# Three small moves in a fused recurrent-attention and MLP kernel: reloads behind a store, the order of the first weights, and a step without a filler

## The chip, the cores and the metric

The kernel runs on one core of one Trainium2 chip. The metric is the time of one execution on the device in microseconds (us); the median over runs is compared. Profiles come from one profiled execution, whose own time is given beside its span.

## What is computed

The output mixes two branches of the same input `x` (2048 rows of 512) with a gate per row. Branch A is attention over segments of 32 rows with 8 memory rows that are carried from segment to segment, so its 64 segments must be computed one after the other. Branch B is a two-layer MLP with a layer norm in front.

```python
def _A_ref(x, mem0, Wq, Wk, Wv, Wo, seg_len):   # 32 heads of 128; M = 8, seg_len = 32
    mem = mem0
    for s in range(n_seg):
        h = concatenate([mem, xs], axis=1)      # 40 rows
        q, k, v = h @ Wq, h @ Wk, h @ Wv        # per head
        p = softmax(where(mask, q @ k.T * scale, -1e9))
        o = (p @ v) @ Wo
        mem = o[:, :M, :]
        outs.append(o[:, M:, :])
def _B_ref(x, w1, b1, w2, b2):
    y = _layernorm(x)
    return gelu(y @ w1 + b1) @ w2 + b2          # 512 -> 1376 -> 512
g = sigmoid((x * gate_w).sum(-1))
return g * a + (1 - g) * b
```

## The kernel before

Everything runs under a manual schedule: the order in which the program calls the instructions is the order on each engine, and the only freedom left is how long each engine waits for the others. Loads that SyncE issues stand in its queue in program order; a wait in front of one holds up all behind it.

**First stage, the MLP (0 to about 86 us).** x is cut into 16 tiles of 128 rows, taken in 8 blocks of two. A block has 11 units `fc`, one for each 128 of the 1376 hidden columns. `a_mm(blk, fc)` does the first layer of a unit: four matmuls into one of two PSUM banks in turn (`SbF` for even units, `W` for odd ones), and a gelu on ScalarE, with the bias column of `b1_sb`, into `hTm`. `b_mm(blk, fc)`, issued two units later (`LAG = 2`), multiplies that with the unit's slice of w2. `prep(blk)` computes the layer norm on VectorE, and `prep_tr` transposes the result `y` on PE; for block 1 this needs the loads of x2 and x3, and its transposes stand behind units 8 and 9 of block 0. The first block also needs w1 in three pieces (units 0 to 2, 3 to 6, 7 to 10: the loads of lines 328, 336 and 337) and w2 (units 0 to 2 and 3 to 5 on ScalarE's queue, line 333; units 6 to 9 by line 339 on SyncE's). Before the first unit PE runs warm-up matmuls on the identity matrix (`warm`, line 521): 13 before the transposes of y, 2 behind them. Then comes the transpose of the bias `b1r` into bank `W` (line 529) and VectorE's copy into `b1_sb` (line 530).

For six of the 16 tiles (`DEF`) the second layer is put off: `spill` stores their gelu results to DRAM (`h_dr`), in 11 pieces of 128 x 128 for each tile.

**The loop (about 86 to 760 us): 64 steps, one for each segment.** A step projects q, k and v (lines 127, 146), computes scores (265, 269) and exponentials (773, 784), sums them over a head's rows with a matrix of ones (`msum`: lines 276, 279), normalises (`mnorm`), multiplies with v (`av`: lines 289, 294), projects with Wo (`wo_pass`: line 158) and takes the new memory rows out of it (`new_mem`: line 728 on PE, 730 on VectorE). Four steps `si` = 0 to 3 make a tile `T`.

Work that doesn't depend on the recurrence fills PE between these parts. Fillers are generators: `run(n)` takes n pieces of the step's own filler (`side`), and `next(mlp)` takes half a unit of the second layer that was put off. `mlp_halves` (line 659 of the profile) multiplies one 128 x 128 piece `hm` of `h_dr` with w2 in two halves of four matmuls into bank `W`; every step takes two halves, one between the matmuls of v and `msum(1)`, one behind `run(W1)`. In step 2, which has no other filler, `mlp_units(7)` takes seven whole units besides, at the places of `run`.

The pieces are loaded by `hm_load` (line 638, SyncE) into five buffers: four ahead of the loop, and one more each time a unit is done, from inside `mlp_halves`. In step 2 four more come with one load into a buffer of another kind (`hm_load4`), which isn't replaced. The two loads of each step that the normalisation of the other rows needs are issued in `recip_x`: the reciprocals `R` are stored to DRAM (`r_dr`, line 699), and read back, spread over all partitions, into `Rb` (line 700); the second waits for the first. One step later POOL multiplies with `Rb` (`x_norm`, line 712) into `UT`, which that step's `wo_pass` reads.

Of the kernel before, what the change touches and what calls it, by code (L numbers as in the profile page):

```python
# [10 lines left out]
BF16 = mybir.dt.bfloat16  # L11
# [16 lines left out]
def kernel(ctx, tc, A_x, A_mem0, A_Wq, A_Wk, A_Wv, A_Wo, A_seg_len, B_x, B_w1, B_b1, B_w2, B_b2, gate_w, out):  # L28
    nc = tc.nc
    P = 128  # L30
# [10 lines left out]
    FC = (F + P - 1) // P  # L41
# [20 lines left out]
    ident = pers.tile([P, P], BF16)  # L62
    g_all = pers.tile([P, NT], FP32)
    omg = pers.tile([P, NT], FP32)
    w2_sb = pers.tile([P, FC, Dm], BF16)
# [147 lines left out]
    def wo_left(T, bk):  # L213
        for n in range(NW):
            wo_group(bk, UL[T % 2], n)
            if n < NW - 1:
                yield

        def ca():
            wl = cw.tile([P, Dm], BF16, tag="wl", name="wl")  # L220
            nc.scalar.copy(out=wl[:], in_=bk[:])
            wls[T] = wl
        act_q.append(ca)
        yield
# [75 lines left out]
    with tc.tile_pool(name="mlpw", bufs=1) as mlpw, \  # L300
# [23 lines left out]
        F0 = 3 * P  # L324
# [2 lines left out]
        w1v = B_w1.rearrange("(kc p) f -> p kc f", p=P)  # L327
        nc.sync.dma_start(w1_sb[:, :, 0:F0], w1v[:, :, 0:F0])

        NWARM = 13  # L330
        H1, H2, F1 = 3, 6, 7 * P
        for a, b in ((0, H1), (H1, H2)):
            nc.scalar.dma_start(w2_sb[:, a:b, :], B_w2[a * P:b * P, :].rearrange("(fc p) d -> p fc d", p=P))
        ld_x(2)
        ld_x(3)
        nc.sync.dma_start(w1_sb[:, :, F0:F1], w1v[:, :, F0:F1])
        nc.sync.dma_start(w1_sb[:, :, F1:F], w1v[:, :, F1:F])
        nc.gpsimd.dma_start(gw_bc[:], gate_w.partition_broadcast(P))
        nc.sync.dma_start(w2_sb[:, H2:FC - 1, :], B_w2[H2 * P:(FC - 1) * P, :].rearrange("(fc p) d -> p fc d", p=P))
        nc.sync.dma_start(w2_sb[:FR, FC - 1, :], B_w2[(FC - 1) * P:F, :])  # L340
        nc.sync.dma_start(w2_sb[FR:FR + 1, FC - 1, :], B_b2.rearrange("(o d) -> o d", o=1))
        ld_x(4)
# [121 lines left out]
        def a_mm(blk, fc):  # L464
            rows = min(P, F - fc * P)
            hp = (SbF, W)[(blk * FC + fc) % 2]
            for kc in range(KC):
                nc.tensor.matmul(hp[:rows, 0:TB * P], lhsT=w1_sb[:, kc, fc * P:fc * P + rows], rhs=yTs[blk][:, kc, :], start=(kc == 0), stop=(kc == KC - 1))  # L468
            nc.scalar.activation(out=hTm[blk % 2][:rows, fc, :], in_=hp[:rows, 0:TB * P], func=ACTF.Gelu_apprx_tanh, bias=b1_sb[:rows, fc:fc + 1], scale=1.0)

        def b_mm(blk, fc):
# [47 lines left out]
        def warm(n):  # L519
            for _ in range(n):  # L520
                nc.tensor.matmul(U[3][:].rearrange("p (a b) -> p a b", a=4), lhsT=ident[:], rhs=ident[:].unsqueeze(1).to_broadcast([P, 4, P]), start=True, stop=True, skip_group_check=True)

        warm(NWARM)
        b1p = W[:].bitcast(BF16)[:, 0:FC]
        prep(0)
        for tt in range(TB):
            prep_tr(0, tt)
        warm(2)
        nc.tensor.transpose(b1p, b1r[:], ident[:FC, :FC])
        nc.vector.tensor_copy(out=b1_sb[:], in_=b1p)  # L530
        side0 = iter(())
        cgen = consts()
        units = [(blk, fc) for blk in range(NBLK) for fc in range(FC)]
# [81 lines left out]
    def side(T, si):  # L615
        gens = []
        if si == 2:
            gens = [wo_left(T - 1, X1) if T >= 1 else mlp_units(7)]
        elif T + 1 < NT:
            gens = [[left_qk(T + 1, 0, 0, X1), left_qk(T + 1, 1, 0, U[3])], [left_qk(T + 1, 0, 1, X1), left_qk(T + 1, 1, 1, U[3])], [],  # L620
                    [left_v(T + 1, 0, X1), left_v(T + 1, 1, U[3])]][si]
        return chain(*gens)
# [30 lines left out]
    def mlp_halves():  # L653
        while hms:
            T, fc, hm, n = hms.pop(0)
            for h in range(2):
                cc = slice(256 * h, 256 * h + 256)
                for c in range(4):
                    nc.tensor.matmul(W[32 * c:32 * c + 32, cc], lhsT=hm[:, 32 * c:32 * c + 32], rhs=w2_sb[:, fc, cc],  # L659
                                     start=(fc == 0 and h == 0), stop=(fc == FC - 1), skip_group_check=True, tile_position=(0, 32 * c))  # L660
                if h == 1:
                    hm_load(n)
                    if fc == FC - 1:
                        mlp_out(T)
                yield

    def mlp_units(n):
        for _ in range(n):
            next(mlp, None)
            next(mlp, None)  # L670
            yield

    hm_load(4)
    mlp = mlp_halves()
    XRs, Rbs = {}, {}
# [18 lines left out]
    def recip_x(s):  # L694
        R = Rs.pop(s)
        nc.vector.reciprocal(out=R[:, 8 * NG:RW], in_=xs8)

        Rb = cw.tile([P, P, NG], FP32, tag="Rb", bufs=1, name="Rb")
        nc.sync.dma_start(r_dr[s % 2][:], R[:, 8 * NG:RW])
        nc.sync.dma_start(Rb[:].rearrange("p r e -> p (r e)"), r_dr[s % 2][:].rearrange("r e -> (r e)").partition_broadcast(P))  # L700
        for i2 in (1, 0):
            nc.vector.tensor_copy(out=R[:, 32 * i2:32 * i2 + 32], in_=RP[i2])  # L702
        mask_put(0)
        nc.gpsimd.tensor_tensor(out=racc[:, 0:RW], in0=racc[:, 0:RW], in1=R[:, 0:RW], op=ALU.add)  # L704
        Rbs[s] = Rb
# [28 lines left out]
    for s in range(nseg):  # L734
# [67 lines left out]
        for kc in range(1, KC - 1):  # L802
            v_unit(X2, hc, 1, kc)
        if not last:
            next(mlp, None)
            msum(1)
            mnorm(1)
        v_unit(X2, hc, 1, KC - 1)
# [2 lines left out]
        if last:  # L811
            break
        run(W1)
        next(mlp, None)
        xsums(E, 1)
        recip_x(s)
        av(s, V, E)
# [197 lines left out]
```

## Time and profile before

| | us |
|---|---|
| median of 3 runs (lowest, highest) | 767.43 (767.12, 767.94) |
| the profiled execution, and its span | 767.13, 765.4 |
| PE busy (share of the span) | 744.7 (97%) |
| ScalarE (ACT), VectorE (DVE), GpSimd (POOL) busy | 537.1, 401.0, 275.1 |
| DMA: bytes moved, mean rate | 74.96 MB, 98 GB/s |

How to read the views: a row of the timeline has its start, its length, the engine (PE the matmuls, PEld the weight loads, and a q behind the name for what an engine's queue issues, SPq for SyncE's), the line, the operation, output `<-` inputs, shapes and how many; in brackets how long the engine stood idle before and what released it. Rows that follow each other closely are merged. In a list of waits a row has who waited for whom, the total us, how many times, and the longest. The chain follows the work that ended last backwards through whatever released each piece. A DMA's time to landing counts from its issue.

### The profile page before, as it was taken

To read this page: it belongs to the slowest core of one execution; us is meant where nothing else is said; L and a number is where in the kernel's file an instruction comes from. 1 tells how busy PE (TensorE), PEld (TensorE's weight loads), DVE (VectorE), ACT (ScalarE), POOL (GpSimd) and SP (SyncE) were. 2 spreads that over 40 slices of the span, in tenths; PEclk is the share of its full clock that TensorE was granted. 3 is DMA by queue.
4 is the path that set the end of the run, shared out by engine and by line. 5 is a ranking of instruction groups with operands and counts; after the bars stand their busy time and mean duration, and the time that the engine had idled before them with its cause. 6 is when DMAs were issued, how large, how long until landed. Compare 5 with 4: busy or idle time off the path is not lost.

```text
span 765.4 us, 44786 instructions
## 1 busy us (share of the span) xinstructions
PE 744.7 (97%) x19624; PEld 423.4 (55%) x19635; DVE 401.0 (52%) x1434; ACT 537.1 (70%) x1625; POOL 275.1 (36%) x517
## 2 busy tenths in 40 slices
PE   8999999999999999999999999999999999999997
PEld 5666455556555555655555655555555555555553
DVE  5876454545555544645455545445454555445444
ACT  4766676777777777777777777777777777677663
POOL 4001133344433334342444333343433444333441
PEclk9999999999999999999999999999999999999999
DMA  8999423212132322222121324222222213222211
GB/s 276 335 305 314 138 76 87 71 59 76 58 94 74 91 66 59 74 83 83 60 78 56 94 66 95 69 56 76 82 78 72 73 56 93 64 83 69 73 57 49
DMA packets 71994, 74.96 MB, mean 98 GB/s; under 512 B 39401, under 2 KB 61906, under 8 KB 70258
## 3 DMA queue, kind: packets, MB, share of 16 engines
q1 hardware_dynamic: 70354, 69.96, 30.1%
q8 instruction: 155, 2.54, 1.4%
q0 software_dynamic: 496, 1.18, 0.5%
q10 hardware_dynamic: 944, 0.92, 0.4%
q14 instruction: 45, 0.37, 0.2%
HBM read 59.13 MB, written 6.62 MB: 86 GB/s over the span
## 4 chain that ended last, share of the span: by engine, by line
PE 93%; DVE 3%; DMA 2%; issue 1%; ACT 1%; SPq 0%; DVEq 0%; ACTq 0%
PE U L127 33%; PE X L158 19%; PE X L146 16%; PE X L127 4%; PE U L289 3%; PE W L468 2%; PE U L475 2%; PE W L659 2%; PE U L146 2%; PE SbF L468 2%; PE U L265 1%; DMA w_sb<-in_B_w_dram 1%; PE U L728 1%; PE SbF L265 1%; PE SbF L685 1%
## 5 line engine op out<-in xcount | busy, mean ns | idle before, releaser
L712 POOL TENSOR_TENSOR UT<-XR,Rb 128x384 bf16<-128x384 bf16 x126 | 140.3, 1137 | 302.0 <-DMA Rb<-r_dr 234.0
L132 ACT CAST Tb<-U 128x512 bf16<-128x512 f32 x288 | 169.0, 587 | 81.7 <-PE U L127 79.1
L127 PEld LDWEIGHTS <-hT 128*32 128x32 bf16 x4096 | 109.5, 96 | 98.7 <-DVE hT L730 8.2
L146 PE MATMUL X<-Wv_sb,hT 128*32 128x512 bf16 x2048 | 144.1, 378 | 0.1
L127 PE MATMUL U<-Wq_sb,hT 128*32 128x512 bf16 x2048 | 137.1, 381 | 0.1
L127 PE MATMUL U<-Wk_sb,hT 128*32 128x512 bf16 x2048 | 133.5, 379 | 0.0
L158 PE MATMUL X<-Wo_sb,UT 128*32 128x512 bf16 x2016 | 122.7, 380 | 1.5 <-ACT UT L819 0.8
L730 DVE CAST hT<-U 128x8 bf16<-128x8 f32 x126 | 21.0, 167 | 168.3 <-PE U L728 126.1
L790 ACT CAST V<-X 128x256 bf16<-128x256 f32 x256 | 88.7, 372 | 16.4 <-PE X L146 3.5
L136 DVE STREAM_TRANSPOSE QT<-Tb 128x256 f32<-128x256 f32 x128 | 56.6, 442 | 73.2 <-ACT Tb L132 72.8
L158 PEld LDWEIGHTS <-UT 128*32 128x32 bf16 x2080 | 56.5, 96 | 60.7 <-issue 17.8
L691 ACT CAST XR<-U 128x256 bf16<-128x256 f32 x252 | 78.4, 433 | 0.0
L719 ACT CAST w<-X 128x128 bf16<-128x128 f32 x189 | 44.7, 309 | 43.6 <-PE X L158 43.6
L136 DVE STREAM_TRANSPOSE KT<-Tb 128x256 f32<-128x256 f32 x128 | 57.0, 445 | 31.1 <-ACT Tb L132 23.2
L712 POOL TENSOR_TENSOR UL<-XR,Rb 128x128 bf16<-128x128 bf16 x126 | 60.5, 504 | 0.0
L146 PEld LDWEIGHTS <-hT 128*32 128x32 bf16 x2048 | 47.1, 94 | 20.5 <-issue 0.2
L704 POOL TENSOR_TENSOR racc<-racc,R 128x72 f32<-128x72 f32 x63 | 21.3, 337 | 102.3 <-DVE R L702 82.1
L819 ACT CAST UT<-U 128x64 bf16<-128x64 f32 x252 | 35.3, 226 | 28.9 <-PE U L294 28.9
L468 PEld LDWEIGHTS <-w_sb 128*128 128x128 bf16 (+1 forms) x352 | 33.3, 100 | 18.6 <-issue 5.5
L773 ACT ACTIVATE E<-U 128x64 bf16<-128x64 f32 (+1 forms) x128 | 35.0, 273 | 11.3 <-PE U L269 11.2
L728 PEld LDWEIGHTS <-w 128*32 128x32 bf16 x1008 | 23.7, 93 | 31.9 <-ACT w L719 25.3
L127 PE MATMUL U<-Wk_sb,GL 128*32 128x512 bf16 x496 | 39.9, 377 | 0.0
(169 smaller groups left out, 1233.3 us busy)
## 6 DMA issues: line engine op xcount, KB each, us to landing
Rb<-r_dr SPq DMA_DIRECT2D x63, 512.0 KB, 4.0
Wv_sb<-in_A_Wv_dram SPq DMA_DIRECT2D x4, 1024.0 KB, 7.4
Wq_sb<-in_A_Wq_dram SPq DMA_DIRECT2D x4, 1024.0 KB, 8.2
Wk_sb<-in_A_Wk_dram SPq DMA_DIRECT2D x4, 1024.0 KB, 8.6
Wo_sb<-in_A_Wo_dram SPq DMA_DIRECT2D x4, 1024.0 KB, 11.1
VP<-VL SPq DMA_DIRECT2D x64, 64.0 KB, 3.3
c<-c_dr SPq DMA_DIRECT2D x16, 128.0 KB, 2.7
hm<-h_dr SPq DMA_DIRECT2D x62, 32.0 KB, 3.3
```

The source lines that it names most:

```text
L127: nc.tensor.matmul(bk[32 * j:32 * j + 32, :], lhsT=G[:, kc, :], rhs=W5[t][:, kc, h0:h1, j, :], start=(kc == 0), stop=(kc == KC - 1), tile_ ...
L132: nc.scalar.copy(out=Tb[:], in_=bk.rearrange("p (a b e) -> p a e b", a=8, b=2))
L136: nc.vector.transpose(out=dst[:, 8 * hf:8 * hf + 8, c0:c0 + 32, :].rearrange("p a r b -> p a (r b)").bitcast(FP32), in_=Tb[:].rearrange("p ...
L146: nc.tensor.matmul(bk[32 * j:32 * j + 32, :], lhsT=G[:, kc, :], rhs=Wv5[:, kc, 4 * vb:4 * vb + 4, j, :], start=(kc == 0), stop=(kc == KC - ...
L158: nc.tensor.matmul(bk[32 * c:32 * c + 32, :], lhsT=U_[:, j, i, :], rhs=Wo_sb[:, 4 * i + j, :], start=(n == 0), stop=(n == NW - 1), tile_po ...
L468: nc.tensor.matmul(hp[:rows, 0:TB * P], lhsT=w1_sb[:, kc, fc * P:fc * P + rows], rhs=yTs[blk][:, kc, :], start=(kc == 0), stop=(kc == KC - 1))
L691: nc.scalar.copy(out=XR[:, j], in_=U[j][:, 0:NG * 40].rearrange("p (i q) -> p i q", q=40)[:, :, 0:32])
L712: nc.gpsimd.tensor_tensor(out=out[:, :, 4 * h:4 * h + 4, o:o + b - a], in0=XR[:, :, 4 * h:4 * h + 4, a:b], in1=Rb[:, h, :, :, a:b], op=ALU ...
L719: nc.scalar.copy(out=w[:, a:b], in_=bk[:, a:b])
L773: nc.scalar.activation(out=E[:, 4 * i2:4 * i2 + 4, c], in_=Sb[i2][:, :, c], func=ACTF.Exp, scale=scale)
L790: nc.scalar.copy(out=V[:, i0:i0 + 2, :].rearrange("p i e -> p (i e)"), in_=(X1, X2)[vb][:, 256 * h:256 * h + 256])
L819: nc.scalar.copy(out=UT[s % 2][:, j, :, 0:M], in_=U[j][:, 0:NG * 40].rearrange("p (i q) -> p i q", q=40)[:, :, 32:40])
```

## The change

- First stage: the second w1 piece is requested right behind the first, ahead of x2 and x3; the second w2 piece goes from ScalarE's queue to SyncE's, behind x3; 12 warm-up matmuls instead of 13 and one instead of two behind the transposes; the transpose of the bias and its copy stand behind the matmuls of the first unit, ahead of its gelu.
- Loop: the first step takes no halves of the second layer; step 2 takes eight units at `run` instead of seven.
- Loop: a unit that is done no longer requests the next piece itself but counts it in `owed`; `recip_x` requests what is owed between the store of the reciprocals and the load of `Rb`.

```diff
@@ -327,16 +327,20 @@
         w1v = B_w1.rearrange("(kc p) f -> p kc f", p=P)
         nc.sync.dma_start(w1_sb[:, :, 0:F0], w1v[:, :, 0:F0])
 
-        NWARM = 13
+        NWARM = 12
         H1, H2, F1 = 3, 6, 7 * P
-        for a, b in ((0, H1), (H1, H2)):
-            nc.scalar.dma_start(w2_sb[:, a:b, :], B_w2[a * P:b * P, :].rearrange("(fc p) d -> p fc d", p=P))
+
+        def ld_w2(eng, a, b):
+            eng.dma_start(w2_sb[:, a:b, :], B_w2[a * P:b * P, :].rearrange("(fc p) d -> p fc d", p=P))
+
+        ld_w2(nc.scalar, 0, H1)
+        nc.sync.dma_start(w1_sb[:, :, F0:F1], w1v[:, :, F0:F1])
         ld_x(2)
         ld_x(3)
-        nc.sync.dma_start(w1_sb[:, :, F0:F1], w1v[:, :, F0:F1])
+        ld_w2(nc.sync, H1, H2)
         nc.sync.dma_start(w1_sb[:, :, F1:F], w1v[:, :, F1:F])
         nc.gpsimd.dma_start(gw_bc[:], gate_w.partition_broadcast(P))
-        nc.sync.dma_start(w2_sb[:, H2:FC - 1, :], B_w2[H2 * P:(FC - 1) * P, :].rearrange("(fc p) d -> p fc d", p=P))
+        ld_w2(nc.sync, H2, FC - 1)
         nc.sync.dma_start(w2_sb[:FR, FC - 1, :], B_w2[(FC - 1) * P:F, :])
         nc.sync.dma_start(w2_sb[FR:FR + 1, FC - 1, :], B_b2.rearrange("(o d) -> o d", o=1))
         ld_x(4)
@@ -466,6 +470,10 @@
             hp = (SbF, W)[(blk * FC + fc) % 2]
             for kc in range(KC):
                 nc.tensor.matmul(hp[:rows, 0:TB * P], lhsT=w1_sb[:, kc, fc * P:fc * P + rows], rhs=yTs[blk][:, kc, :], start=(kc == 0), stop=(kc == KC - 1))
+            if blk == 0 and fc == 0:
+                b1p = W[:].bitcast(BF16)[:, 0:FC]
+                nc.tensor.transpose(b1p, b1r[:], ident[:FC, :FC])
+                nc.vector.tensor_copy(out=b1_sb[:], in_=b1p)
             nc.scalar.activation(out=hTm[blk % 2][:rows, fc, :], in_=hp[:rows, 0:TB * P], func=ACTF.Gelu_apprx_tanh, bias=b1_sb[:rows, fc:fc + 1], scale=1.0)
 
         def b_mm(blk, fc):
@@ -521,13 +529,10 @@
                 nc.tensor.matmul(U[3][:].rearrange("p (a b) -> p a b", a=4), lhsT=ident[:], rhs=ident[:].unsqueeze(1).to_broadcast([P, 4, P]), start=True, stop=True, skip_group_check=True)
 
         warm(NWARM)
-        b1p = W[:].bitcast(BF16)[:, 0:FC]
         prep(0)
         for tt in range(TB):
             prep_tr(0, tt)
-        warm(2)
-        nc.tensor.transpose(b1p, b1r[:], ident[:FC, :FC])
-        nc.vector.tensor_copy(out=b1_sb[:], in_=b1p)
+        warm(1)
         side0 = iter(())
         cgen = consts()
         units = [(blk, fc) for blk in range(NBLK) for fc in range(FC)]
@@ -615,7 +620,7 @@
     def side(T, si):
         gens = []
         if si == 2:
-            gens = [wo_left(T - 1, X1) if T >= 1 else mlp_units(7)]
+            gens = [wo_left(T - 1, X1) if T >= 1 else mlp_units(8)]
         elif T + 1 < NT:
             gens = [[left_qk(T + 1, 0, 0, X1), left_qk(T + 1, 1, 0, U[3])], [left_qk(T + 1, 0, 1, X1), left_qk(T + 1, 1, 1, U[3])], [],
                     [left_v(T + 1, 0, X1), left_v(T + 1, 1, U[3])]][si]
@@ -659,7 +664,7 @@
                     nc.tensor.matmul(W[32 * c:32 * c + 32, cc], lhsT=hm[:, 32 * c:32 * c + 32], rhs=w2_sb[:, fc, cc],
                                      start=(fc == 0 and h == 0), stop=(fc == FC - 1), skip_group_check=True, tile_position=(0, 32 * c))
                 if h == 1:
-                    hm_load(n)
+                    owed[0] += n
                     if fc == FC - 1:
                         mlp_out(T)
                 yield
@@ -670,6 +675,7 @@
             next(mlp, None)
             yield
 
+    owed = [0]
     hm_load(4)
     mlp = mlp_halves()
     XRs, Rbs = {}, {}
@@ -697,6 +703,8 @@
 
         Rb = cw.tile([P, P, NG], FP32, tag="Rb", bufs=1, name="Rb")
         nc.sync.dma_start(r_dr[s % 2][:], R[:, 8 * NG:RW])
+        hm_load(owed[0])
+        owed[0] = 0
         nc.sync.dma_start(Rb[:].rearrange("p r e -> p (r e)"), r_dr[s % 2][:].rearrange("r e -> (r e)").partition_broadcast(P))
         for i2 in (1, 0):
             nc.vector.tensor_copy(out=R[:, 32 * i2:32 * i2 + 32], in_=RP[i2])
@@ -802,7 +810,8 @@
         for kc in range(1, KC - 1):
             v_unit(X2, hc, 1, kc)
         if not last:
-            next(mlp, None)
+            if s:
+                next(mlp, None)
             msum(1)
             mnorm(1)
         v_unit(X2, hc, 1, KC - 1)
@@ -811,7 +820,8 @@
         if last:
             break
         run(W1)
-        next(mlp, None)
+        if s:
+            next(mlp, None)
         xsums(E, 1)
         recip_x(s)
         av(s, V, E)
```

## The prediction

> **What bounds the kernel now.** I read the page first, then PE's list of waits, then the timeline of the first 18 us, of step 0 and of step 2 of the loop, and last the queue of SyncE.
>
> ```profile
> span 765.4 us, 44786 instructions
> ...
> PE 744.7 (97%) x19624; PEld 423.4 (55%) x19635; DVE 401.0 (52%) x1434; ACT 537.1 (70%) x1625; POOL 275.1 (36%) x517
> ...
> GB/s 276 335 305 314 138 76 87 71 59 76 58 94 74 91 66 59 74 83 83 60 78 56 94 66 95 69 56 76 82 78 72 73 56 93 64 83 69 73 57 49
> ...
> PE 93%; DVE 3%; DMA 2%; issue 1%; ACT 1%; SPq 0%; DVEq 0%; ACTq 0%
> ```
>
> PE is busy 97% of the span and carries 93% of the chain that ended last. A change that leaves PE's work alone can win only where PE stands still. The chain gives 2% to DMA, and PE's own list of waits names two places, once each:
>
> ```profile
> PE W L659 <- DMA hm<-h_dr: 1.2, 1, 1.2
> ...
> PE W L468 <- DMA w_sb<-in_B_w_dram: 0.6, 1, 0.6
> ```
>
> The change works on both. The profiled execution took 767.13 us, 1.73 more than its span; the median of the three runs is 767.43, so I add the difference of the sum to 767.43. A measurement of this kernel can tell about 0.2% (1.5 us) from no change.
>
> **The start: transfers and PE's order.**
>
> ```profile
> 1.47 5.73 PE L521 MATMUL U<-ident 128*128 128x512 bf16 x13 [1.47 <-POOL ident masks.py:199]
> ...
> 1.68 0.97 SPq L315 DMA_DIRECT2D xt<-in_A_x_dram  x2
> ...
> 2.69 0.48 SPq L336 DMA_DIRECT2D w_sb<-in_B_w_dram  x1
> ...
> 7.00 0.75 PE L447 MATMUL X<-ident,y 128*128 128x128 bf16 x8
> ...
> 8.11 0.18 PE L529 MATMUL W<-ident,b1r 11*128 11x11 bf16 x1
> ...
> 8.33 0.17 DVE L530 COPY b_sb<-W 128x11 bf16<-128x11 bf16 x1
> 8.37 0.60 PE L468 MATMUL SbF<-yT,w_sb 128*128 128x256 bf16 x4
> 8.41 0.68 DVE L428 BATCH_NORM_STATS2 st<-xt 128x6 f32<-128x512 bf16 x1
> ...
> 9.01 0.47 ACT L469 ACTIVATE hTm<-SbF,b_sb 128x256 bf16<-128x256 f32 x1 [1.66 <-PE SbF L468]
> ...
> 9.44 0.47 ACT L469 ACTIVATE hTm<-W,b_sb 128x256 bf16<-128x256 f32 x1
> ...
> 10.99 0.61 PE L468 MATMUL W<-yT,w_sb 128*128 128x256 bf16 x4 [0.65 <-DMA w_sb<-in_B_w_dram]
> ...
> 12.51 0.73 DVE L440 TENSOR_SCALAR y<-xt,mv,rs 128x512 bf16<-128x512 bf16 x2
> ...
> 14.70 0.38 PE L475 MATMUL U<-w_sb,hTm 128*128 128x512 bf16 x1
> ...
> 14.91 0.39 PE L447 MATMUL X<-ident,y 128*128 128x128 bf16 x4
> ```
>
> The chain in order of time has one transfer here, and the view of line 339 gives the landing of another:
>
> ```profile
> 2.69 8.25 DMA w_sb<-in_B_w_dram
> ```
>
> ```profile
> L339 SPq DMA_DIRECT2D w_sb<-in_B_w_dram x1: 527/527/527, 4.0 to 4.0; - x1
> ...
> DMA to landing us min/median/max: 9.7/9.7/9.7
> ```
>
> Unit 3 of the first layer (10.99) waited for the second piece of w1, issued at 2.69, landed at 10.94. The change issues it at 1.68, before x2 and x3, and takes half of the early w2 off ScalarE's queue, which competed with it (ScalarE has its issue, some 0.5 us, less; it is idle there). Even with the same 8.25 us it lands at 9.93; with 0.4 MB less in front I expect about 8.3. So this wait ends. What is late next?
>
> *ScalarE's pace.* Units alternate two banks, so unit 3 needs the gelu of unit 1: 9.44 + 0.47 = 9.91, PE about 9.96. But the change also moves the bias transpose behind unit 0's matmuls, in bank W, which unit 1 writes. One warm-up matmul less (5.73 / 13 = 0.44) lets the transposes of y (7.00) start up to 0.4 earlier, hence unit 0 at about 8.05 (8.37 less 0.3). Its four matmuls take 0.43 (8.80 came 0.43 after 8.37), the bias transpose to the end of its copy 0.39 (8.11 to 8.50): the bias is there at about 8.9, and unit 1 and gelu 0 start then, against 8.80 and 9.01. Gelu 1 follows unit 1 by 0.64 (9.01 − 8.37), at about 9.5, and unit 3 starts at 10.1. Gain there: 0.9, bounds 0.8 and 1.0. Fewer warm-ups and the moved bias cost nothing by themselves because 10.94 hid them; that cover is gone, and this is why the gain isn't 1.4.
>
> *The w2 piece of line 339*, used first at 14.70, lands at 4.0 + 9.7 = 13.7. The bytes ahead of it are the same as before, only reordered, so I leave its landing there. It would allow a gain of 1.0, so it is no worse than ScalarE's pace.
>
> *x2 and x3*, now behind 0.5 MB more. Ahead of the end of x3 lie x0 to x3 (0.52 MB), three weight pieces of 0.39, 0.39 and 0.52 MB: 1.83 MB, at the first slice's 276 GB/s 6.6 us, from about 2 us on: 8.6. The statistics of x2 start now at 8.41, then behind the bias copy at about 8.9; y of x2 and x3 is used at 14.91, and the first is ready 4.5 us after its statistics start (12.51 and half of 0.73, less 8.41): 13.4, wanted at 14.0. If x2 landed as late as 10.3, 0.9 us would be lost and the gain with it. The w2 piece moved from ScalarE's to SyncE's queue goes ahead of w1's last; it is first used by second-layer unit 3, about 11.8, and should be in by 10.5. I take 0.9 for the start, bounds 0 and 1.3. From there the chain is PE, and DVE links that hang on PE's transposes, so it carries through.
>
> **Step 0: no unit.**
>
> ```profile
> 89.15 2.80 SPq L638 DMA_DIRECT2D hm<-h_dr  x4
> ...
> 90.89 0.61 PE L146 MATMUL X<-Wv_sb,hT 128*32 128x512 bf16 x8
> ...
> 91.17 0.23 ACT L773 ACTIVATE E<-U 128x64 bf16<-128x64 f32 x1 [0.17 <-PE U L269]
> ...
> 92.73 0.29 PE L659 MATMUL W<-w_sb,hm 128*32 128x256 bf16 x4 [1.23 <-DMA hm<-h_dr]
> ...
> 92.85 0.19 PE L276 MATMUL U<-E,BO 128*32 128x32 bf16 x4
> ```
>
> The same places two steps on, where nothing is awaited:
>
> ```profile
> 112.88 0.61 PE L146 MATMUL X<-Wv_sb,hT 128*32 128x512 bf16 x8
> ...
> 113.16 0.22 ACT L773 ACTIVATE E<-U 128x64 bf16<-128x64 f32 x1 [0.17 <-PE U L269]
> ...
> 113.43 0.20 PE L276 MATMUL U<-E,BO 128*32 128x32 bf16 x4
> ```
>
> The stored activations are asked for at 89.15 and stop PE until 92.73, with the sums (L276) queued behind them. Without the half unit the sums wait for the exponentials only. In step 2 they start 0.05 after those end (113.38); in step 0 that is 91.40 + 0.05 = 91.45 instead of 92.85: 1.40. Behind them DVE's normalisation and ScalarE's casts of V keep their own length, so the 0.1 us of the other half unit is mostly filler: I take 1.35, bounds 1.2 and 1.6. Of SyncE's queue one load leaves this step; nothing new waits.
>
> **Step 2: eight units.** The chain there:
>
> ```profile
> 117.81 0.23 PE W L659 x7
> ...
> 118.06 0.22 PE SbF L728 x8
> ```
>
> The moved unit goes between these two rows' small matmuls, where PE stands still for no more than 0.02 us: +0.21 (0.23 − 0.02).
>
> **The loads behind the store.**
>
> ```profile
> 115.07 0.38 SPq L699 DMA_DIRECT2D r_dr<-R  x1
> ```
>
> ```profile
> L638 SPq DMA_DIRECT2D hm<-h_dr x62: 319/578/2174, 89.2 to 652.3; - x62
> ...
> DMA to landing us min/median/max: 1.9/3.3/5.1
> ```
>
> ```profile
> SPq L700 <- DMA r_dr<-R: 82.4, 63, 2.7
> ```
>
> ```profile
> Rb<-r_dr SPq DMA_DIRECT2D x63, 512.0 KB, 4.0
> ```
>
> SyncE waits 82.4 / 63 = 1.31 us for each store before it may issue Rb. One load's issue, 0.58, fits in; at worst 2.17 − 1.31 = 0.9 comes on top, and 32 KB ahead of 512 KB on the way a sixteenth of 4.0, 0.25. So Rb may come up to 1.1 us later. Who waits for it: POOL's normalisation, then PE's output projection. The nearest of the 54 steps with loads:
>
> ```profile
> 132.48 2.22 POOL L712 TENSOR_TENSOR UT<-XR,Rb 128x384 bf16<-128x384 bf16 x2 [5.39 <-DMA Rb<-r_dr]
> ```
>
> ```profile
> 136.01 1.26 PE L158 MATMUL X<-Wo_sb,UT 128*32 128x512 bf16 x20
> ```
>
> POOL is done 1.31 us before PE starts, so 1.1 costs nothing. In front of the store, the loads had delayed it hardly ever, so nothing is won either. The data is used three steps later, except in step 2: its last unit wants a piece requested behind that step's own store. Issued at 115.45 it is wanted at 118.05, 2.6 later. With only a 4 KB store in front I take a landing near 1.9: no cost; at 3.3 it costs 0.7.
>
> **Sum:** −0.90 − 1.35 + 0.21 = −2.04; 767.13 becomes 765.09, and the median 767.43 − 2.04 = 765.4.
>
> **Rivals.**
> 1. *The first stage gives nothing* (0.10). The warm-ups run at 0.44 us each, the same matmul later at 0.21 to 0.22 in the chain: PE starts at half pace. With two warm-ups less, full pace could come later; the units of 8.05 to 11 at half pace lose 1.3 us, or x2 is late by the 0.9 worked out above. Time: 767.43 − 1.35 + 0.21 = 766.3. Against it: twelve warm-ups still cover 1.5 to 6.7. The Trainium skill (TensorE: Matmul & The Clock Gate, Part 1) says full clock comes after some 3.4 us of sustained work in a free-running window, and that the number of matmuls is not what counts; by that rule the change is harmless here, though the thirteen at 0.44 (5.73 us) show that it can take longer than 3.4.
> 2. *Step 2 waits for its last piece* (0.17). At 3.3 us to landing: 765.4 + 0.7 = 766.1. For it: the median; against it: that median holds loads queued behind Rb.
> 3. *The loads push Rb out* (0.07), the slower side. If Rb's data came only once the load has landed, Rb is late by about the load's 3.5 us less the 1.31 of waiting: 2.2. Summed over the 54 steps, what lies over each step's margin (1.31 in the row above, most between 2 and 3.7) is 4.7 us; below 1.3 it is nothing, at 1.9 it eats the gain. Time: 765.4 + 4.7 = 770.1. Against it: Rb waits for the store alone.
>
> **Numbers.** The forecast has 0.66: 765.4, own range 764.6 to 766.0. If the start gives 1.3 and step 0 1.6 it is 764.7, and with the scatter of the runs 764.4. Up to 766.8 it takes in rivals 1 and 2 with the same scatter; rival 3 is left out. Faster by over 0.2% means below 765.9: most of the forecast and a third of rival 2, 0.66; within 0.2%: 0.27; slower 0.07.
>
> **What would show it.** Right: no wait of PE on a transfer of w1, unit 3 near 10.1, the first bias copy near 8.9; L276 of step 0 0.05 behind its exponentials; Rb issued within 1.5 us of most stores. Wrong: PE waiting on w2 or y before 15 us, on hm at the end of step 2, or on POOL before L158.

## The result, and the profile after

Changed kernel: 763.81 us median over 20 runs (761.48 to 766.32). The kernel before, in the same sitting: 765.97 over 20 runs (763.15 to 767.94), with the three runs shown among them. The ratio is 0.9974, with a 95% interval of 0.9963 to 0.9986: 2.0 us less, between 1.1 and 2.8. The forecast of the difference was −2.04. The forecast of the time, 765.4 with a range of 764.4 to 766.8, missed.

The profiled execution of the changed kernel took 762.26 us. The head of its page, and PE's list of waits, in which neither transfer that the prediction quoted is left:

```profile
span 760.5 us, 44799 instructions
...
PE 744.4 (98%) x19633; PEld 421.5 (55%) x19633; DVE 402.8 (53%) x1434; ACT 537.1 (71%) x1625; POOL 275.1 (36%) x517
...
PE 93%; DVE 3%; DMA 1%; ACT 1%; issue 1%; SPq 0%; DVEq 0%; ACTq 0%
```

```profile
PE U L289 <- issue: 2.1, 6, 0.6
...
PE W L472 <- ACT hTm L477: 1.4, 2, 1.0
```

In the first, PE waits for nothing that the trace names: "issue". In the profile of before that row was twice as large:

```profile
PE U L289 <- issue: 4.1, 10, 0.6
```

*The start.* The timeline of the changed kernel (line numbers are 4 to 8 higher than before):

```profile
8.57 0.17 DVE L476 COPY b_sb<-W 128x11 bf16<-128x11 bf16 x1 [0.80 <-PE W L475]
...
9.42 0.47 ACT L477 ACTIVATE hTm<-W,b_sb 128x256 bf16<-128x256 f32 x1 [0.18 <-PE W L472]
...
9.80 0.69 DVE L432 BATCH_NORM_STATS2 st<-xt 128x6 f32<-128x512 bf16 x1 [1.07 <-DMA xt<-in_A_x_dram]
...
9.95 0.60 PE L472 MATMUL W<-yT,w_sb 128*128 128x256 bf16 x4
...
13.21 0.60 PE L472 MATMUL SbF<-yT,w_sb 128*128 128x256 bf16 x4
...
13.91 0.73 DVE L444 TENSOR_SCALAR y<-xt,mv,rs 128x512 bf16<-128x512 bf16 x2
13.95 0.38 PE L483 MATMUL U<-w_sb,hTm 128*128 128x512 bf16 x1
14.38 0.40 PE L451 MATMUL X<-ident,y 128*128 128x128 bf16 x4
```

Unit 3 starts at 9.95 (10.99 before), without a wait for w1, right behind the gelu of unit 1 (9.42 + 0.47). But VectorE stood still until x2 landed at 9.78 and starts its statistics at 9.80 (8.41 before); the transposes of y come at 14.38 instead of 14.91. Of the 1.04 won at unit 3, 0.53 is left. (x2's landing: 2.23 + 7.55 in the row below.) The chain's transfer is no longer w1 but x2:

```profile
2.23 7.55 DMA xt<-in_A_x_dram
```

There is a second late transfer. L483 at 13.95 is the second layer's unit 6, the first to use the w2 piece of units 6 to 9 (line 334 here, line 339 before). The changed kernel asks for that piece at 4.62, and it lands at 13.91. Behind matmuls that start at 13.21 this unit would start at about 13.64, as 12.99 follows 12.55 for the unit before; it starts 0.04 behind the landing instead. So w2 costs some 0.3 us here, and the wait for y another 0.2 on top (14.38 instead of 13.95 + 0.22).

*Step 0.* The sums follow the exponentials at 0.06 (90.64 + 0.22 = 90.86, then 90.92):

```profile
90.64 0.22 ACT L781 ACTIVATE E<-U 128x64 bf16<-128x64 f32 x1 [0.17 <-PE U L269]
...
90.92 0.20 PE L276 MATMUL U<-E,BO 128*32 128x32 bf16 x4
...
92.75 1.47 PE L158 MATMUL X<-Wo_sb,UT 128*32 128x512 bf16 x24
```

L276 is 1.93 earlier than before (92.85): 0.53 of the start and 1.40 of the step. The output projection of step 0 (L158, 92.75) is my landmark from here on; in the profile of before its row starts at 94.68.

### The profile page after: what moved, and what is told of

It is laid out like the page before. It is cut to its first block, busy times and chain, and to the rows that moved or that the text cites. A ratio compares the mean times of both kernels' runs of the same rounds, so it can differ in the third digit from the quotient of the medians.

```text
span 760.5 us, 44799 instructions
## 1 busy us (share of the span) xinstructions
PE 744.4 (98%) x19633; PEld 421.5 (55%) x19633; DVE 402.8 (53%) x1434; ACT 537.1 (71%) x1625; POOL 275.1 (36%) x517
## 4 chain that ended last, share of the span: by engine, by line
PE 93%; DVE 3%; DMA 1%; ACT 1%; issue 1%; SPq 0%; DVEq 0%; ACTq 0%
PE U L127 33%; PE X L158 19%; PE X L146 17%; PE X L127 4%; PE U L289 3%; PE U L483 2%; PE U L146 2%; PE W L664 2%; PE W L472 2%; PE SbF L472 1%; PE U L265 1%; DMA xt<-in_A_x_dram 1%; PE U L736 1%; PE SbF L265 1%; PE SbF L691 1%
## 5 line engine op out<-in xcount | busy, mean ns | idle before, releaser
L127 PEld LDWEIGHTS <-hT 128*32 128x32 bf16 x4096 | 107.4, 96 | 100.7 <-DVE hT L738 8.2
L158 PE MATMUL X<-Wo_sb,UT 128*32 128x512 bf16 x2016 | 121.6, 380 | 0.8 <-ACT UT L829 0.8
L158 PEld LDWEIGHTS <-UT 128*32 128x32 bf16 x2080 | 57.0, 96 | 58.3 <-issue 16.5
L146 PEld LDWEIGHTS <-hT 128*32 128x32 bf16 x2048 | 46.9, 94 | 20.9 <-issue 0.4
```

Of the source, the lines that this page charges most:

```text
L127: nc.tensor.matmul(bk[32 * j:32 * j + 32, :], lhsT=G[:, kc, :], rhs=W5[t][:, kc, h0:h1, j, :], start=(kc == 0), stop=(kc == KC - 1), tile_ ...
L146: nc.tensor.matmul(bk[32 * j:32 * j + 32, :], lhsT=G[:, kc, :], rhs=Wv5[:, kc, 4 * vb:4 * vb + 4, j, :], start=(kc == 0), stop=(kc == KC - ...
L158: nc.tensor.matmul(bk[32 * c:32 * c + 32, :], lhsT=U_[:, j, i, :], rhs=Wo_sb[:, 4 * i + j, :], start=(n == 0), stop=(n == NW - 1), tile_po ...
```

## The experiments

Each number in the table below is of one profiled execution. "Step 0" is the start of the output projection of step 0. "4 to 62" is the distance between the starts of the output projections of steps 4 and 62; a step without a stall takes 10.23 us, every fourth 10.46, which makes 596.7, and what lies above that is the stray time.

| kernel | step 0 | 4 to 62 |
|---|---|---|
| before, first profile; a second one | 94.68; 94.37 | 607.51; 602.86 |
| changed, first profile; a second one | 92.75; 92.60 | 604.17; 604.24 |
| the new start alone | 93.62 | 604.17 |
| no unit in step 0 alone | 93.02 | 604.55 |
| pieces behind the store alone | 93.20 | 603.01 |
| changed, gate load later; a second one | 92.06; 91.99 | 603.49; 605.14 |
| that, masks where VectorE idles; a second one | 90.46; 90.63 | 605.87; 604.62 |
| that, pieces behind Rb | 90.57 | 605.14 |
| changed, 78 more instructions | 93.40 | 605.06 |

Steps 0 to 4, which lie between the two columns, take 41.33, 42.26 and 42.06 us in the three profiles with the whole loop of before, 41.66 and 43.55 in the two of the changed kernel. Scatter of the size of the whole gain lies there too.

**One part of the change at a time.** The new start with the loop of before:

```
keeps: w1 piece ahead of x2, x3; w2 piece on SyncE; 12 and 1 warm-ups; bias behind unit 0
undoes: owed[0] += n          -> hm_load(n), in mlp_halves
        if s: next(mlp, None) -> next(mlp, None)    (both places)
        mlp_units(8)          -> mlp_units(7)
```

> Only the first stage is changed; the loop is the one of before. Theory A (the parts add up, each worth its own wait): the transposes of y of block 1 start at 14.4 us instead of 14.91, unit 3 near 9.95 instead of 10.99; in step 0 PE still waits on hm, the sums (L276) start about 92.3 instead of 92.85 (0.5 earlier); median 0.5 us below before. Theory B (the loads behind the store or the order in the loop shortens the steps 4 to 62): the time stays within 0.5 us of before and these steps take as long as before, 607.5 us, against 604.2 in the profile of the changed kernel. Theory C (the steps' scatter has nothing to do with the change): these steps take anything from 603 to 609 us, the excess at every third step.

Measured: 763.35 against 764.58, ratio 0.9982 [0.9968, 0.9996].

Step 0 without its unit, all else as before:

```
-  next(mlp, None)          # both places in the step
+  if s: next(mlp, None)
-  mlp_units(7)
+  mlp_units(8)
```

> Only the unit of the first step is moved into step 2; first stage and place of the loads are those of before. Theory A: L276 of step 0 starts 0.05 us behind its exponentials, at 91.45 instead of 92.85 (1.4 us earlier); step 2 is 0.2 longer; median 1.2 us below before. Theory B: nothing in steps 4 to 62 (607.5 us), so only 1.2 of the 4.9 us between the two profiles. Theory C: steps 4 to 62 anywhere from 603 to 609 us.

Measured: 763.02, ratio 0.9982 [0.9968, 0.9996].

The pieces behind the store, all else as before:

```
-  hm_load(n)                       # in mlp_halves
+  owed[0] += n
   nc.sync.dma_start(r_dr[s % 2][:], R[:, 8 * NG:RW])
+  hm_load(owed[0]); owed[0] = 0    # in recip_x
```

> Only the loads of the pieces are moved behind the store of the reciprocals. Theory A: no change of time (within 0.3 us of before, in the middle of the runs); step 0 keeps its wait of 1.2 us on hm; Rb issued 1.4 to 2.4 us after the store, 3 to 4 in step 3 where three loads are owed. Theory B: steps 4 to 62 come down from 607.5 to about 604 us and the median by 2 to 3 us. Theory C: steps 4 to 62 anywhere from 603 to 609, median as before.

Measured: 764.33, ratio 0.9995 [0.9978, 1.0011]: no difference that can be told.

The two kernels that keep the unit in step 0 also show how long PE waits there for its first piece. First the new start alone, then the pieces behind the store alone (the second has the same order of SyncE's queue up to that point as the kernel before):

```profile
88.57 2.84 SPq L643 DMA_DIRECT2D hm<-h_dr  x4
...
91.67 0.29 PE L664 MATMUL W<-w_sb,hm 128*32 128x256 bf16 x4 [0.77 <-DMA hm<-h_dr]
```

```profile
88.75 2.86 SPq L638 DMA_DIRECT2D hm<-h_dr  x4
...
90.92 0.29 PE L659 MATMUL W<-w_sb,hm 128*32 128x256 bf16 x4
91.03 0.20 PE L276 MATMUL U<-E,BO 128*32 128x32 bf16 x4
```

In the second PE doesn't wait at all. So a second profile of the kernel before was taken.

> The kernel before, unchanged, profiled once more. Theory (the wait of step 0 and the stray stalls of TensorE are properties of an execution, not of the kernel's order alone): the wait of the MLP matmuls of step 0 on their first piece is anywhere between 0 and 1.3 us (1.23 in the first profile, 0.77 and 0 in the profiles that keep the old loads and the old units in that step), and the distance from wo_pass of step 4 to that of step 62 is 603.0 to 604.7 us as in the other profiles, not 607.5 again. Rival (the first profile is typical of this kernel): the wait is 1.2 us again and the distance 607 to 608 us. Time 763 to 768 us.

```profile
89.34 2.83 SPq L638 DMA_DIRECT2D hm<-h_dr  x4
...
92.43 0.29 PE L659 MATMUL W<-w_sb,hm 128*32 128x256 bf16 x4 [0.74 <-DMA hm<-h_dr]
```

764.07 us, and the wait is 0.74 here. Four executions with the unit in step 0 gave 1.23, 0.74, 0.77 and 0: 0.69 in the mean. The wait that the prediction takes away is a matter of the execution; the first profile held the longest. The kernels without that unit load the piece as well, so all 14 profiles tell its landing: 3.0 to 3.6 us after its issue in 12 of them, and 1.6 in two, one of which is the profile without a wait. That one is rare, then, and a mean over four that includes it is rather low. What sets the landing from one execution to the next was not found.

The changed kernel once more, on the chip of this second profile:

> The changed kernel, unchanged, timed and profiled once more beside the two kernels below. Theory: 0.9970 to 0.9985 of before, its profile within 0.5 us of the first one at every landmark up to the step 4 (unit 3 at 9.9, the first row-block's transposes of block 1 at 14.4, the first value matmul of step 0 at 90.9) as long as the third and the fourth tile of x land as late as before (9.8). Rival: the start moves by the time at which those tiles land; then the landmarks move by as much.

762.76 against 764.86, ratio 0.9970 [0.9956, 0.9983]. x2 came at 9.16 here, 0.6 sooner than in the first profile, and the transposes of y at 14.21, with everything ahead of them 0.23 later. Here y is ready in time (13.30 and half of 0.73), and what holds up PE is the w2 piece: it lands at 13.95, and unit 6 starts at 13.99. The profile of the new start alone shows that wait by name:

```profile
14.10 0.38 PE L483 MATMUL U<-w_sb,hTm 128*128 128x512 bf16 x1 [0.21 <-DMA w_sb<-in_B_w_dram]
```

```profile
4.79 9.27 DMA w_sb<-in_B_w_dram
```

In all five profiles with the new start and the gate's load (below) in its place, unit 6 starts 0.04 us behind the landing of that piece (13.77 to 14.13). So w2 sets the gain of the start in four of them, and x2, in the first profile, takes 0.2 more. The gain differs from one execution to the next at the other end as well: in four profiles of the old start, w1's second piece lands at 10.94, 11.08, 10.58 and 10.52, and the transposes of y start at 14.91, 15.05, 14.55 and 14.50. Their mean is 14.75, that of the five of the new start 14.26: 0.5 us.

**Why x2 and the w2 piece are late.** GpSimd asks for the gate's weights, one row of 1 KB spread over 128 partitions, ahead of all this. The issue, and then the bandwidth by stretches, in the changed kernel (start:end, length, busy times of PE, PEld, DVE, ACT and POOL, PE's clock, DMA share, GB/s):

```profile
3.53 0.58 POOL L342 DMA_DIRECT2D gw_bc<-in_gate_w_dram  x1
```

```profile
6.00:7.50 1.50, 1.50 (x11) 0.56 (x10) 1.31 (x5) 1.34 (x2) 1.50 (x10) 1.00 1.10 383
7.50:9.00 1.50, 0.94 (x8) 0.66 (x7) 0.44 (x2) 0.23 (x1) 1.44 (x10) 1.00 0.99 197
9.00:10.50 1.50, 1.50 (x14) 1.16 (x12) 0.69 (x1) 1.19 (x3) 0.47 (x2) 1.00 1.03 354
```

Between 7.5 and 9 the DMA engines are about as busy as before and after (share 0.99) and move half as much. By queues, in that stretch, most of their time goes to GpSimd's queue, q0, whose only load then is this one (packets, MB, share):

```profile
q0 software_dynamic: 37, 0.11, 64.1%
q1 hardware_dynamic: 193, 0.18, 35.2%
```

The next kernel moves that load alone:

```
-  nc.gpsimd.dma_start(gw_bc[:], gate_w.partition_broadcast(P))   # issued at 3.53
+  the same, behind GpSimd's masks                                # issued at 8.39
```

> The changed kernel with the load of the gate weights (one row of 1 KB read 128 times) issued on POOL about 5 us later. Theory D (this load holds up what is on the way, which is why x2, whose last packet left at 7.6, landed only at 9.8): x2's statistics start at 8.8 instead of 9.80, y's transposes (L451, second group) at 13.85 instead of 14.38, unit 6 of the second layer at 13.7 instead of 13.95; median 0.5 us below the changed kernel. Theory E (x2 is late because 0.5 MB of w1 is in front of it): x2's statistics stay at 9.8 and the transposes at 14.4, no change.

```profile
7.50:9.00 1.50, 1.09 (x9) 0.82 (x9) 0.70 (x3) 0.40 (x1) 1.41 (x7) 1.00 1.09 382
```

```profile
8.48 0.68 DVE L433 BATCH_NORM_STATS2 st<-xt 128x6 f32<-128x512 bf16 x1
...
13.69 0.39 PE L452 MATMUL X<-ident,y 128*128 128x128 bf16 x4
```

The dip is gone from there; another lies at 12.5 to 13.5 now (96 and 155 GB/s in its halves), where the w2 piece has landed (12.11). The statistics of x2 start 1.32 sooner than in the changed kernel, the transposes of y 0.69 sooner, 0.17 of which PE has already at unit 3 (9.78). The w2 piece tells the two orders apart best: it lands at 13.8 to 14.1 in the five profiles with the gate load in its place and at 12.1 to 13.1 in the five with it moved, where PE doesn't wait for it. x2 doesn't tell them apart as well: 7.9 to 9.8 with the load in its place, though the dip is in all five profiles, and 8.0 to 8.9 with it moved. So the load alone doesn't explain how late x2 was in the first profile. In the kernel before, the same load in the same stretch leaves 326 GB/s of 380. 760.6 against 764.58, ratio 0.9942 [0.9930, 0.9955]. The time was measured again later, on another chip:

> The changed kernel with the gate-weights load moved alone, once more, beside the others. Theory: 0.9942 of before as in the first measurement, within 0.9930 to 0.9960; the first stage is 0.6 to 0.8 us shorter than the changed kernel's and 1.6 us longer than that of the kernel above. Rival: the 760.6 of the first measurement were five lucky runs, and it is 762 to 763, as much below the changed kernel as the first stage says.

761.6 against 764.61, ratio 0.9963 [0.9948, 0.9978]. That is nearer to the rival of that expectation than to its theory: the five runs of the first measurement lay on the low side. Its first stage is 0.6 to 0.7 us shorter than the changed kernel's, and that much and no more can be put down to it.

**The next wait of that stage.** With the gate load out of the way, PE waits 1.00 us at 19.26 for a gelu, behind a gate product, behind eight small VectorE instructions that build masks.

```
   consts(): yields after 4, 6 and then every 3 instructions (was 8, then 4 and 4 ...)
+  next(cgen, None)                      # ahead of unit 0 of block 0
-  if fc == 9: next(cgen, None)
+  if fc == f0: next(cgen, None)         # between the two transposes of a block
```

> The changed kernel with the gate-weights load 5 us later on GpSimd's queue (as in the run before) and, in addition, the 24 small VectorE instructions that build the masks handed out three or so at a time where VectorE idles in the first stage, instead of 8 in block 0 and 4 each in blocks 1 to 4 ahead of the gates. Theory (after the gate load, the next limit of the first stage is VectorE's queue ahead of the gates: TensorE waited 1.00 us at 19.26 and 0.46 us at 27.58 for a GELU behind a gate product behind these instructions): both waits go or shrink to under 0.3, the first value matmul of step 0 comes 0.8 to 1.4 us before its 90.23, and the time is 759.2 to 759.8. Rival (those waits are ScalarE's backlog of GELUs and stay): 760.4 to 760.8, no different from the run with the gate load moved alone (760.6).

The waits before (gate load later alone) and with this:

```profile
19.26 0.60 PE L473 MATMUL W<-yT,w_sb 128*128 128x256 bf16 x4 [1.00 <-ACT hTm L478]
27.58 0.60 PE L473 MATMUL SbF<-yT,w_sb 128*128 128x256 bf16 x4 [0.46 <-ACT hTm L478]
```

```profile
18.37 0.60 PE L477 MATMUL W<-yT,w_sb 128*128 128x256 bf16 x4 [0.21 <-ACT hTm L482]
26.44 0.60 PE L477 MATMUL SbF<-yT,w_sb 128*128 128x256 bf16 x4 [0.21 <-ACT hTm L482]
```

The output projection of step 0 comes 1.4 to 1.6 us sooner than with the gate load moved alone, as expected or a little more. The time: 761.75 against 764.86, ratio 0.9939 [0.9916, 0.9961]; in its median the expected 759.2 to 759.8 was missed by two. In the first pair of profiles the later steps lose it again (605.87 against 603.49), in the second they don't (604.62 against 605.14), so where it went isn't shown. Again beside the kernel without it:

> The kernel with the gate-weights load later and the masks built where VectorE idles, once more, beside the two below. Theory (its first stage is 1.6 us shorter than with the gate load moved alone): 1.0 to 1.8 us below that kernel in median, 0.993 to 0.994 of before. Rival (what the first stage wins is lost in stray stalls): the same time as that kernel.

761.12 against 761.6: ratios 0.9945 [0.9924, 0.9966] and 0.9963 [0.9948, 0.9978]. The shorter first stage is shown, the shorter time isn't: the intervals overlap. By ratio this is the best version that was run, some 4 us under the kernel before.

**When does Rb cost something?** Six more loads of 32 KB, into scratch, between the store and Rb in every step:

```
   hm_load(owed[0])
+  for k in range(6):
+      nc.sync.dma_start(scr[k], h_dr[1][k])
```

> The changed kernel with six more loads of 32 KB (DRAM to DRAM, into scratch that nobody reads) issued between the store of the reciprocals and Rb in every step: tests at what delay Rb costs time. Theory (Rb has a margin of 2.45 us in the median step of the changed kernel, 1.4 in the smallest of the later steps, and only what lies beyond it costs): six issues of 0.58 us, of which about 0.5 still fit into the wait for the store, push Rb out by 2.9 us; summed over the margins of the profile that is +27 us (+12 at 2.5, +46 at 3.3), and TensorE waits before the output projection, on the normalised x. Rival (any load between the two costs its own length, so that the loads behind the store cost already): 63 times 3.5, +200 us or so. Second rival (Rb isn't on any path that matters): within 1 us of the changed kernel.

815.79 us, ratio 1.0646 [1.0601, 1.0690]. Rb is issued 5.40 us behind the store in the median step (1.59 in the changed kernel), 3.8 later and not 2.9. PE now waits for POOL's normalisation, which waits for Rb, in its matmuls and in their weight loads:

```profile
POOL UT L723 <- DMA Rb<-r_dr: 270.2, 38, 9.1
...
PEld L158 <- POOL UT L723: 35.0, 56, 1.8
...
PE X L158 <- POOL UT L723: 13.5, 21, 1.3
```

So rival 3 names a real path. POOL is done 2.45 us ahead of PE in the median step of the changed kernel; a delay of 3.8, and a landing of Rb that takes 4.3 us instead of 3.9, costs some 50 us, while the loads of the change, which leave the median delay of Rb where it was (1.55 before, 1.59 after), cost nothing that shows. The expectation took the delay a quarter too small and so the cost by half (27 us); its sum over the margins, at 3.8, would give some 75 to 80, which is too much. Delays between these two were not tried, so where the cost begins isn't measured.

The opposite end: on top of the masks version, the pieces behind Rb from step 3 on.

```
+  if s == 2: hm_load(owed[0]); owed[0] = 0
   nc.sync.dma_start(Rb[:]...)
+  hm_load(owed[0]); owed[0] = 0
```

> As the kernel with the masks where VectorE idles, but from step 3 on the pieces are requested behind Rb and no longer between the store and Rb (step 2 keeps them ahead of Rb). Theory (Rb's margin covers the pieces in all steps but step 3, where three are owed at once): Rb issues 1.45 to 1.6 us after the store in all steps, the wait of step 3 on the normalised x (0.2 to 0.5 us) goes, nothing else changes: 0 to 0.5 us less, not to be told from the same kernel without it. Rival (the loads ahead of Rb cost in many steps): 1.5 us less or more.

761.32, ratio 0.9956 [0.9940, 0.9971], no different from the same kernel without it (0.9945). But the wait of step 3 did not go, against the expectation:

```profile
122.44 1.64 SPq L711 DMA_DIRECT2D r_dr<-R  x1
...
125.28 0.32 SPq L715 DMA_DIRECT2D Rb<-r_dr  x1
125.65 1.37 SPq L649 DMA_DIRECT2D hm<-h_dr  x3
...
131.13 2.19 POOL L729 TENSOR_TENSOR UT<-XR,Rb 128x384 bf16<-128x384 bf16 x2 [7.56 <-DMA Rb<-r_dr]
```

Rb is 2.84 behind the store although nothing of the pieces stands between, and then takes until 131.1 to be there. What holds it up in step 3 isn't the three pieces' place in SyncE's queue; the burst of stores, loads and a transposing load of that step is a candidate that wasn't tried.

**The stray stalls.** In every profile PE loses up to 1.2 us in some of the steps 4 to 61, mostly in every third, within the value matmuls (L289, L294), and the trace names no releaser. If the place in the instruction stream sets it, 78 more instructions ahead of everything move it:

```
-  for _ in range(n):      one 512-column warm-up matmul
+  for k in range(4 * n):  one 128-column warm-up matmul   # 13 become 52, each with its weight load
```

> The changed kernel with each of its 13 warm-up matmuls cut in four short ones (same columns in all): 78 more TensorE instructions ahead of everything else, nothing else moved. Theory (a step whose value matmuls start at an instruction count of about 66 to 134 modulo 256 loses 0.25 to 0.55 us to a stall that shows as issue, whatever its work): the stalls leave the steps 3k that have them in the changed kernel's profile and turn up in steps 3k+2 (2, 5, 8, 11 and so on); the sum from step 4 to step 62 stays at 6 to 9.5 us, and the time within 1.5 us of the changed kernel's. Rival A (the stalls belong to the work of steps 3k, a transfer or another engine's work that repeats every three steps): they stay in steps 3k. Rival B (they are random in an execution): no pattern.

Rows of step 36 of the changed kernel (its second profile), and of step 20 of this one:

```profile
469.30 0.20 PE L289 MATMUL U<-E,V 32*128 32x40 bf16 x5 [0.70 <-issue]
```

```profile
303.22 0.20 PE L289 MATMUL U<-E,V 32*128 32x40 bf16 x4 [0.79 <-issue]
```

The 40 value matmuls of a step take 0.32 us in the median step, from the start of the first to that of the last. What they take beyond that, summed over steps 5 to 61 by the step's number modulo 3: in the changed kernel 5.56, 0.39 and 0.30 us for 0, 1 and 2 (second profile 5.71, 0.33, 0.32); with the 78 instructions 0.61, 0.31 and 6.05. They moved, as the theory has it, from 3k to 3k+2. Matching the records of the value matmuls with the program's order gives the very instruction that is late, as its count from the start among matmuls and weight loads, modulo 256:

```
before           step 12: 168   24: 156   36: 144   48: 132
changed          step 12: 168   24: 156   36: 144   48: 132
78 more          step  8: 172   20: 160   32: 148   44: 136
```

Count and step add up to 180 in each, though the matmul that this hits is another one in each kernel (in step 12 the 26th of the 40 value matmuls before, the 28th in the changed kernel); the drift of one a step is a semaphore instruction that PE's list has in each step and that this count leaves out. With the semaphore instructions counted, the late matmul is number 194 or 195 modulo 256, counted from 0, in every one of the 104 stalls of over 0.15 us without a releaser that the value matmuls have in the 14 profiles, of ten different kernels. Every 256 instructions there is one place where PE may stand, and it does so where that place falls among these short matmuls. The Trainium skill (Runtime: NRT & Kernel Launch, Instruction fetch mechanics) says that an engine's instructions are refetched in blocks of 16 KiB, 256 instructions, at a cost that is mostly hidden. The period of 256 agrees; the cost, if it is that, is not hidden here, 0.2 to 0.4 us in the mean of the 19 steps it falls on in these five profiles. The traces show an instruction queue (q8) that moves 155 packets of 16 KB, and in them each of the 35 such stalls ends 1.2 to 1.6 us behind the end of one of them. That the stall is the fetch itself isn't shown: it is the reading that fits the period.

The time did not behave: 765.75, against 762.76 for the changed kernel on the same chip, where I allowed 1.5. The stray time of steps 4 to 62 grew by only 0.8 in the profile, and its step 0 is 0.8 late for a stall on the exponentials; the rest of the 3.0 is not explained.

## Why the prediction was right or wrong

**The base: wrong, and this is the step that failed.** "The median of the three runs is 767.43, so I add the difference of the sum to 767.43." Three runs that agree within 0.8 us looked like a base. In 20 runs this kernel lies anywhere between 763.15 and 767.94, with a median of 765.97, and 764.58, 764.86 and 764.61 in three later sittings on three different chips; the three lay in the upper part of that. With 765.97 as its base the same sum gives 763.93, where 763.81 was measured. The range was built on the scatter of the three ("with the scatter of the runs": 0.3 down, 0.5 up) and so was too narrow as well as 1.5 too high. The profile had the sign: its own stray stalls, 10.8 us above the plain steps between steps 4 and 62, where the second profile of the same kernel has 6.2. The prediction shows 1% of the chain as "issue", and no term of it has a price for that. Why the first three runs were slower than most of the others stays open.

**w1 and unit 3: right.** No wait on w1; unit 3 at 9.95 (forecast 10.1); the bias copy at 8.57 to 8.74 (8.9). ScalarE's pace set it, as worked out.

**w2 and x2: wrong by size.** The prediction left the landing of the w2 piece at 13.7 because "the bytes ahead of it are the same as before", and found it no worse than ScalarE's pace. It landed at 13.8 to 14.1 in five profiles, and PE waited for it in each. x2 was taken to be in by 8.6 at 276 GB/s, with 10.3 as the bound; 9.78 came in the first profile, 9.16 in the second. The bandwidth was no constant: 383, then 197 GB/s while the gate load ran, then 354. So the transposes of y came 0.53 sooner in the first profile and 0.70 in the second, 0.5 by the means over nine profiles, not 0.90; "PE waiting on w2 or y before 15 us", a sign of being wrong, came. The 4.5 us from x2's statistics to y were right (9.80 to 14.28), and the path by which x2 would cost was the one named under rival 1. Rival 1's other arm, PE at half pace without the two warm-ups, did not come: the units of 9.29 and 9.95 follow each other at 0.66.

**Step 0: right for this pair of profiles, 1.40 against 1.35; too much for the kernel.** From the first sums of step 0 to its output projection the four executions with the unit take 4.01, 3.52, 3.54 and 2.94 us, the changed kernel 2.60 in both of its profiles: taking the unit out was worth 0.3 to 1.4, 0.9 in the mean.

**Step 2: right.** In the chain, two rows of the second layer stand where there was one (+0.23; 0.21 was taken), and no wait for the last piece, so rival 2 fell in this execution. It is a real one all the same: in the profile with 78 more instructions, whose loop is that of the changed kernel, PE waits 0.43 us for that piece. Pieces land 2.1 us after their issue in the median (3.3 before; 1.9 was taken). The chain, then the row of that wait, then the view of the line in the changed kernel:

```profile
116.09 0.23 PE W L664 x7
...
116.34 0.23 PE W L664 x7
116.57 0.04 PE SbF L736 x7
```

```profile
118.13 0.40 PE L664 MATMUL W<-w_sb,hm 128*32 128x256 bf16 x8 [0.43 <-DMA hm<-h_dr]
```

```profile
DMA to landing us min/median/max: 1.7/2.1/3.8
```

**The loads behind the store: right in sum, wrong in one bound.** "At worst 1.1 later" forgot that the steps without halves leave three pieces owed in step 3:

```profile
124.27 0.38 SPq L705 DMA_DIRECT2D r_dr<-R  x1
124.75 2.55 SPq L643 DMA_DIRECT2D hm<-h_dr  x3
128.00 0.32 SPq L708 DMA_DIRECT2D Rb<-r_dr  x1
```

Rb came 3.73 behind the store (2.34 to 2.41 before, but 3.42 in the new start alone, where no piece stands between), and PE's weight loads waited 0.18 us for POOL there. The median delay is 1.59 (1.55 before), a little over the "within 1.5" of the prediction. That nothing more is lost elsewhere is borne out by the kernel with the pieces behind Rb, which is no faster.

**The sum.** By parts that the profiles showed: −0.5 to −0.7 for the start, −0.9 for step 0 in the mean, +0.2 for step 2 and up to +0.2 in step 3: −1.0 to −1.4. Measured was −2.0 [−2.8, −1.1] and, in the sitting of its second profile, −2.3 [−3.4, −1.3]. That −2.04 was met is thus partly luck: the parts come to half or two thirds of it, just at the small end of these intervals. The three parts measured by themselves, −1.4, −1.4 and −0.4 us, each with ±1 or more, don't settle it. Whether 0.6 to 1.3 us remain, and what they are, stays open; the place of the stalls in the instruction stream moves the time by more than that (3.0 us with 78 more instructions), but that it did so here was not shown.

## What to carry to other kernels

Before a difference of 0.3% is put on a base, ask for the scatter of the base: three runs and one profile are one sample of waits that come and go, and a wait seen once (here 1.2 us, then 0.7, then none) is priced by its mean. When a transfer is moved to the front, look at what else uses the queues in those microseconds, small spread-out loads above all; moving one of them was worth as much in the first stage (0.6 to 0.7 us) as the reordering. When one wait goes, look at each transfer that comes next, and at when it is issued in the new order: the w2 piece was asked for 0.6 us later than before and became the next wait. A stall that the trace gives to nobody may belong to the count of instructions, and can be found by matching the late instruction with its place in the program.

## What was not expected of the hardware

- While one load of 1 KB spread over 128 partitions runs on GpSimd's queue, all queues together move half as much for some 1.5 us (383 to 197 GB/s in the changed kernel; 380 to 326 in the kernel before) at an unchanged share of busy time; with that load moved, the dip moved with it (96 GB/s from 12.5 to 13.0).
- PE stalls at one place in every 256 instructions, by up to 1.2 us, where this falls among short matmuls: some 5 to 9 us of an execution of 764, and different from one to the next.
- The landing of the first of four 32 KB loads after the first stage varies between 1.6 and 3.6 us after its issue.
